# The second layer of a fused attention and snake-activation network: eight units of 576 tokens, and six of 768

## The chip, the cores and the metric

The kernel runs on one core of a Trainium2 chip. The metric is the device time of that core in microseconds, the median of three runs. In the trace PE is TensorE's matmul stream and PEld its loads of stationary operands; DVE is VectorE, ACT ScalarE, POOL GpSimd; SP issues most of the transfers, and ACT issues a few.

## The reference

```python
def _attn_ref(q, k, v):                      # 8 batches, 8 heads, 576 positions, 64 wide
    k_p = k.reshape(B, H, Sp, pool, D).mean(axis=3)
    v_p = v.reshape(B, H, Sp, pool, D).mean(axis=3)
    scores = scale * np.matmul(q, k_p.transpose(0, 1, 3, 2))
    attn = softmax(scores)
    return np.matmul(attn, v_p)
def _moe_ref(x, w_in, w_out, alpha):         # 4608 tokens, 512 -> 2048 -> 512
    h = x @ w_in
    s = np.sin(alpha * h)
    g = h + s * s / (alpha + 1e-09)
    return (g @ w_out).astype(np.float32)
```

All of it is float32. The change concerns the last line alone: `g @ w_out`, a product of 4608 x 2048 by 2048 x 512.

## The kernel before

The first part (`hidden`, `attention`, up to about 514 us) makes g and stores it, transposed, in a scratch tensor `gd` in device memory (`store_g`, L1074). The matmuls of `x @ w_in` have line L848; their moving operand has 256 columns.

The second part is the generator `outputs` (L1290). It takes the 4608 tokens in 8 units of `S` = 576, one for each batch. A unit is one product by a fast scheme of 7 multiplications in place of 8 (Winograd's form of Strassen's), applied twice: an outer level with seven operands numbered 1 to 7 in the `ORDER` 1, 2, 4, 6, 7, 5, 3, and within each of them an inner level with seven again. So a unit has 49 inner products. Each of these adds up four matmuls in PSUM (`product`, L1340), and the profile lists two hardware passes for each float32 matmul: 392 passes a unit, 3136 in all. The moving operand has `T` = `S` / 4 = 144 columns.

The four blocks of a unit's g are loaded by `load_g` (L1286) as tiles r11, r12, r21, r22 (128 partitions x 2304 elements, 1152 KB each). The outer operands are sums of them, made on DVE by `outer`, all with line L1295, since `tt` is defined there: x5 = r21 + r22, x6 = x5 - r11, x7 = r11 - r21 (in r21's place), x3 = r12 - x6; operands 1, 2 and 4 are r11, r12 and r22 as they are. With x5, x6 and x3 these are seven large tiles. For each outer operand `inner` makes four sums s1 to s4 of 576 elements (L1295 too), one product ahead of the matmuls that use them.

The loop at L1427 runs over the (unit, product) pairs, one step for each. A step's stream on PE is: inner product 1 of this pair, then 5 and 4 of the pair before, 6 of this, 2 and 3 of the pair before, 7 of this. (In the first two steps the order differs a little: the first step is mixed into the end of the first layer.) Within the same step DVE gets, in this order: the outer sum that is due, s1 to s3 for the next pair, `combine` of the pair before, s4. So DVE, which works strictly in this order, is tied to PE through `combine`, which reads PSUM.

`combine` (L1370) puts a product's result into the output blocks ca, cb, cc, cd of the pool `op`. Four times a unit `out` (L1357) turns a block by a DVE transpose (L1362) into a tile o (3 buffers) and issues four transfers to the output (L1367, 72 KB each), on SP's queue, and in the last unit on SP's and ACT's in turn (`both`).

The loads of the next unit are all issued on SP's queue: r11, r12 and r22 in the step of product n = 3, r21 in that of n = 5. For unit 0, r11, r12 and r22 are loaded while the first layer still runs (L1560), since their places are free; r21 lies in the pool `gs`, which opens only when the first layer's pools close, and is issued on ACT's queue behind the first layer's last activations (L1571).

Of the kernel before, what the change touches and what calls it, by code (L numbers as in the profile page):

```python
# [40 lines left out]
class Kernel:  # L41
    def __init__(self, tc, q, k, v, w_in, w_out, alpha, out):
        self.tc, self.nc = tc, tc.nc
        self.q, self.k, self.v = q, k, v
        self.w_in, self.w_out, self.alpha, self.out = w_in, w_out, alpha, out
        self.B, self.H, self.S, self.D = q.shape
        self.Sp = self.S // POOL
        self.DM = self.H * self.D
        self.FF = w_in.shape[1]
        self.K1 = self.DM // P  # L50
        self.K2 = self.FF // P
        self.NP = self.H // 2
        self.NU = self.B * self.S // (2 * TH)
        self.NJ = self.K2 // 2 // JW
        self.xT, self.shifts = {}, []
        self.T = self.S // 4

        self.gd = self.nc.dram_tensor("g_bridge", (2, self.NJ * JW, P, self.B * self.S), F32, kind="Internal").ap()

# [1217 lines left out]

    def load_g(self, u, names):  # L1280
        for n in names:
            i, j = divmod(("r11", "r12", "r21", "r22").index(n), 2)
            shape = [P, self.NJ, JW, 2, self.T]
            t = (self.gs if n == "r21" else self.gq if n == "r22" else self.gp).tile(shape, F32, name=n)[:]
            t0 = u * self.S + i * 2 * self.T
            (self.nc.scalar if u == 0 and n == "r21" else self.nc.sync).dma_start(out=t.rearrange("p J b i c -> p (J b) (i c)"),  # L1286
                                   in_=self.gd[j, :, :, t0:t0 + 2 * self.T].rearrange("b p c -> p b c"))
            self.R[n] = t

    def outputs(self):  # L1290
# [9 lines left out]
        def outer(u, n):  # L1300
            r = self.R
            if n == 0:
                X[u] = {1: r["r11"], 2: r["r12"], 4: r["r22"]}
                return
            new = lambda p: self.gs.tile([P, self.NJ, JW, 2, T], F32, name=f"x{p}")[:]
            x = X[u]
            if n == 1:
                x[5] = new(5)
                tt(flat(x[5]), flat(r["r21"]), flat(x[4]), OP.add)
            if n == 2:  # L1310
                x[6] = new(6)
                tt(flat(x[6]), flat(x[5]), flat(x[1]), OP.subtract)
            if n == 3:
                x[7] = r["r21"]
                tt(flat(x[7]), flat(x[1]), flat(x[7]), OP.subtract)
            if n == 4:
                x[3] = new(3)
                tt(flat(x[3]), flat(x[2]), flat(x[6]), OP.subtract)

        def inner(u, n):  # L1320

            x = X[u][ORDER[n]]
            e = self.ne
            self.ne = not e
            new = lambda i: (self.gs if e and i > 1 else self.gq).tile([P, self.NJ, T], F32, name=f"s{i}{int(e)}")[:]
            s1, s2 = new(0), new(1)
            a = lambda i, j: x[:, :, j - 1, i - 1, :]
            tt(s1, a(2, 1), a(2, 2), OP.add)
            tt(s2, s1, a(1, 1), OP.subtract)
            yield  # L1330
            s3, s4 = new(2), new(3)
            tt(s3, a(1, 1), a(2, 1), OP.subtract)
            A[u, n] = {1: a(1, 1), 2: a(1, 2), 3: s4, 4: a(2, 2), 5: s1, 6: s2, 7: s3}
            yield
            tt(s4, a(1, 2), s2, OP.subtract)
# [10 lines left out]
        def early(st):  # L1346

            t = C[st["u"]]["c"]
            with_z(t, st["yz"])
            add(t[:, :, 1], t[:, :, 1], st["x1"][:])  # L1350
            if st["u"] == self.B - 1:
                out(st["u"], 0, 1, t, 5, queues=both)

        def with_z(t, z):
            add(t[:, 1], t[:, 1], z[:, 1:2, :].to_broadcast([P, 2, T]))

        def out(u, i, j, t, n0=0, n1=2 * T // 32, queues=4 * (nc.sync,)):  # L1357

            if n0 or n1 * 32 == 2 * T:
                C[u]["o"] = self.op.tile([P, 2 * T // 32, 2, 32], F32, name="o", bufs=3)  # L1360
            o = C[u]["o"]
            nc.vector.transpose(out=o[:, n0:n1].rearrange("p n h c -> p h n c"),  # L1362
                                in_=t[:].rearrange("p h i c -> p h (i c)").rearrange("p h (n c) -> p h n c", c=32)[:, :, n0:n1])
            r = u * self.S + i * 2 * T
            for a in range(4):
                c = j * 2 * P + a * 64
                queues[a].dma_start(out=self.out[r + 32 * n0:r + 32 * n1, c:c + 64].rearrange("(n k) c -> k n c", k=32),  # L1367
                                        in_=o[32 * a:32 * a + 32, n0:n1].rearrange("k n h c -> k n (h c)"))

        def combine(st):  # L1370

            u, p, x, z = st["u"], st["p"], (st["x0"], st["x1"]), st["yz"]
            c = C.setdefault(u, {})

            def with_x(o, t):
                for i in range(2):
                    add(o[:, :, i], t[:, :, i], x[i][:])
            if p in (1, 4, 5):

                n = "a" if p == 1 else "b"  # L1380
                t = c[n] = block("c" + n)
                for i in range(2):
                    nc.scalar.copy(out=t[:, :, i], in_=x[i][:])
                with_z(t, z)
                if p == 5 and u < self.B - 1:
                    add(c["a"][:], c["a"][:], t[:])
                    out(u, 1, 1, c["a"])
                    add(c["c"][:], c["c"][:], t[:])
                elif p == 5:
                    nc.gpsimd.tensor_tensor(out=c["c"][:], in0=c["c"][:], in1=t[:], op=OP.add)  # L1390
                    add(c["a"][:], c["a"][:], t[:])
                    later.append(lambda: out(u, 1, 1, c["a"], queues=both))
            elif p == 2:
                o = block("cd")
                with_x(o, c["a"])
                with_z(o, z)
                out(u, 0, 0, o)
            elif p == 6:

                t = c["c"] = block("cc")  # L1400
                with_x(t, c["a"])
                with_z(t, z)
            elif p == 7:

                t = c["a"]
                with_x(t, c["c"])
                with_z(t, z)
                add(c["b"][:], c["b"][:], t[:])
                out(u, 1, 0, c["b"])
            else:  # L1410
                t = c["c"]
                add(t[:, :, 0], t[:, :, 0], x[0][:])
                if u < self.B - 1:
                    out(u, 0, 1, t)
                else:
                    out(u, 0, 1, t, 0, 5, both)

        both = 2 * (nc.sync, nc.scalar)
        later = []
        last = None  # L1420
        seq = [(u, n) for u in range(self.B) for n in range(7)]
        outer(0, 0)
        A = {}
        for _ in inner(0, 0):
# [2 lines left out]
        for k in range(len(seq) + 1):  # L1427
            st = None
            if k < len(seq):
                u, n = seq[k]  # L1430
                st = {"u": u, "p": ORDER[n], "A": A.pop((u, n))}
                if 0 < n < 5 and k != 1:
                    outer(u, n)
                if n == 3 and u + 1 < self.B:
                    self.load_g(u + 1, ("r11", "r12", "r22"))
                if n == 5 and u + 1 < self.B:
                    self.load_g(u + 1, ("r21",))
                if n == 6 and u + 1 < self.B:
                    outer(u + 1, 0)
                x0 = st["x0"] = self.bank([P, 2, T])  # L1440
                yz = st["yz"] = self.abank([P, 2, T])
# [51 lines left out]
    def run(self):  # L1493
        nc, tc = self.nc, self.tc
        pool = lambda s, n, b, **kw: s.enter_context(tc.tile_pool(name=n, bufs=b, **kw))
        with ExitStack() as top:
            const = self.const = pool(top, "const", 1)
            self.tp = pool(top, "tp", 1)
            self.PS = pool(top, "ps", 1, space=PSUM).tile([P, 8, 512], F32, name="PS")
            self.aturn = 0  # L1500
            full = self.full = const.tile([P, P], mybir.dt.bfloat16, name="full")
# [3 lines left out]
            engines = {nc.tensor.engine, nc.vector.engine, nc.scalar.engine, nc.gpsimd.engine, nc.sync.engine}  # L1505
            self.wq = pool(top, "wq", 1)
            with ExitStack() as one:
                self.wp = pool(one, "wp", 1)
                self.hp = pool(one, "hp", 2)
                self.xq = pool(one, "xq", 1)  # L1510
                homes = one.enter_context(ExitStack())
                self.xp = pool(homes, "xp", 1)
                att = one.enter_context(ExitStack())
# [31 lines left out]
                for u in range(self.NU):  # L1545
# [8 lines left out]
                            x[i].append(lambda: next(w))  # L1554
                    elif u > self.B - 1:
                        homes.close()
                        self.gq = pool(top, "gq", 1, side="right")
                        for i in (6, 10, 13, 14, 17, 20):
                            x[i].append(lambda: next(w))
                        x[5].append(lambda: self.load_g(0, ("r11", "r12", "r22")))  # L1560
                        for i, f in zip((23, 25, 25, 27), self.inner_w(5, None)):
                            x[i].append(f)
                        o = self.outputs()
                        for i in (22, 25, 27):
                            x[i].append(lambda: next(o))
                    self.hidden(u, x)
                self.end_hidden()
            self.gs = pool(top, "gs", 1, reuse_waits="tile")
            self.op = pool(top, "op", 1, reuse_waits="tile")
# [39 lines left out]
```

## Time and profile before

| | us |
|---|---|
| median of 3 runs | 902.47 (902.22 to 903.03) |
| the profiled execution, its own time | 902.87 |
| its span in the trace | 901.0 |
| PE busy | 894.6 |
| DVE busy | 678.0 |
| ACT busy | 447.9 |
| POOL busy | 212.5 |

A row of the timeline has the start and the length in microseconds, the engine, the line of the source, the operation, output <- input and the count of instructions merged into it; the square brackets say how long the engine was idle before it and who released it. "s" is any inner sum, "r" any loaded tile, "x" any outer operand with a tile of its own. A row of the chain of waits has start, length, engine and line. A row of a table by stages has the stretch, its length, and for each engine the busy time in it and in brackets the number of instructions, then the granted clock, the share of the DMA engines' time and the rate in GB/s. The granted clock of TensorE is 1.00 in all of them.

### The profile page before, as it was taken

How to read it: one execution, taken by the hardware profiler on the slowest of the kernel's cores; microseconds unless marked ns; L12 is line 12 of the kernel's file. 1: busy time of each engine (PE TensorE's matmuls, PEld its weight loads, DVE VectorE, ACT ScalarE, POOL GpSimd, SP SyncE). 2: the span in 40 equal slices, each digit the busy share in tenths (PEclk: the TensorE clock that was granted, in tenths of full speed). 3: DMA queues.
4: the chain of work that ended last, by engine and by line, in shares of the span. 5: the costliest groups of instructions: out<-in, count | busy, mean ns of one | idle time of the engine just before them, and what ended most of it. 6: DMA issues, size and time to landing. Idle time of an engine off the chain costs nothing.

```text
span 901.0 us, 17940 instructions
## 1 busy us (share of the span) xinstructions
PE 894.6 (99%) x7010; PEld 816.3 (91%) x7010; DVE 678.0 (75%) x1010; ACT 447.9 (50%) x1071; POOL 212.5 (24%) x218
## 2 busy tenths in 40 slices
PE   9999999999999999999999999999999999999998
PEld 5787888888888888888888999999999999999997
DVE  7776867768576675764558799979798888889895
ACT  5687776877768777687976611211111111111111
POOL 5698443825337262430000000000000000000000
PEclk9999999999999999999999999999999999999999
DMA  9957957759586585557226346261618172534401
GB/s 264 245 153 206 243 146 210 189 164 253 139 222 184 180 222 145 171 158 282 94 82 223 101 146 191 66 191 35 224 30 230 31 201 64 172 92 127 138 15 40
DMA packets 128371, 141.13 MB, mean 157 GB/s; under 512 B 46416, under 2 KB 95328, under 8 KB 128288
## 3 DMA queue, kind: packets, MB, share of 16 engines
q1 hardware_dynamic: 125504, 137.88, 53.4%
q10 hardware_dynamic: 2784, 2.11, 0.9%
q8 instruction: 56, 0.92, 0.5%
q14 instruction: 27, 0.22, 0.1%
HBM read 75.37 MB, written 47.19 MB: 136 GB/s over the span
## 4 chain that ended last, share of the span: by engine, by line
PE 97%; DVE 2%; DMA 1%; SPq 0%; issue 0%; ACT 0%; DVEq 0%
PE PS L848 46%; PE PS L1340 41%; PE PS L1038 3%; PE PS L317 2%; PE PS L612 2%; PE PS L625 1%; DMA h<-in_v_dram 1%; DVE x L1295 1%; DVE s L1295 0%; DVE r L1295 0%; PE PS L568 0%; PE PS L570 0%; PE PS L289 0%; PE PS L278 0%; PE PS L478 0%; SPq L164 0%
## 5 line engine op out<-in xcount | busy, mean ns | idle before, releaser
L848 PE MATMUL PS<-home,a 128*128 128x256 f32 x1104 | 258.1, 381 | 0.1
L848 PEld LDWEIGHTS PS<-home,a 128*128 128x128 f32 x1104 | 205.3, 190 | 32.3 <-issue 4.6
L848 PE MATMUL PS<-home,as 128*128 128x256 f32 x768 | 182.6, 381 | 0.0
L848 PEld LDWEIGHTS PS<-home,as 128*128 128x128 f32 x768 | 141.8, 190 | 19.7 <-ACT PS L822 1.2
L1390 POOL TENSOR_TENSOR cc<-cc,cb 128x576 f32<-128x576 f32 x1 | 2.0, 1977 | 501.7 <-DVE cb L1295 501.7
L1340 PE MATMUL PS<-s,wb 128*128 128x144 f32 x896 | 119.1, 286 | 0.0
L1340 PEld LDWEIGHTS PS<-s,wb 128*128 128x128 f32 x896 | 113.7, 190 | 0.1
L1015 ACT ACTIVATE s<-s,c 128x256 f32<-128x256 f32 (+1 forms) x228 | 113.5, 565 | 0.0
L821 DVE TENSOR_TENSOR h<-PS,p 128x512 f32<-128x512 f32 x72 | 49.3, 684 | 64.0 <-PE PS L848 37.4
L131 POOL TENSOR_TENSOR kvin<-kvin 96x768 f32<-96x768 f32 (+3 forms) x42 | 73.8, 1756 | 70.3 <-DMA kvin<-in_v_dram 68.1
L1468 ACT COPY PS<-PS 128x144 f32<-128x144 f32 x56 | 14.7, 263 | 145.0 <-PE PS L1340 138.4
L1008 ACT ACTIVATE s<-h,al 128x256 f32<-128x256 f32 x144 | 65.6, 509 | 38.3 <-DVE h L821 38.3
L1340 PE MATMUL PS<-r,wb 128*128 128x144 f32 x512 | 73.3, 286 | 0.3 <-DVE r L1295 0.3
L1340 PE MATMUL PS<-s,a 128*128 128x144 f32 x512 | 73.2, 286 | 0.0
L1008 ACT ACTIVATE s<-PS,al 128x256 f32<-128x256 f32 x144 | 60.2, 471 | 18.8 <-PE PS L848 17.9
L1060 DVE TENSOR_TENSOR h<-PS,s 128x512 f32<-128x512 f32 x36 | 24.8, 689 | 57.4 <-ACT s L1015 57.4
L1340 PEld LDWEIGHTS PS<-r,wb 128*128 128x128 f32 x512 | 67.1, 190 | 0.5 <-DVE r L1295 0.5
L1340 PEld LDWEIGHTS PS<-s,a 128*128 128x128 f32 x512 | 67.1, 190 | 0.0
L822 ACT COPY PS<-PS 128x512 f32<-128x512 f32 x72 | 41.5, 576 | 35.4 <-PE PS L848 30.6
L1488 ACT COPY PS<-PS 128x144 f32<-128x144 f32 x56 | 14.7, 263 | 88.1 <-PE PS L1340 88.1
L1340 PE MATMUL PS<-x,wb 128*128 128x144 f32 x384 | 54.9, 286 | 0.0
L1340 PE MATMUL PS<-s,we 128*128 128x144 f32 x384 | 54.9, 286 | 0.0
(216 smaller groups left out, 1407.5 us busy)
## 6 DMA issues: line engine op xcount, KB each, us to landing
g_bridge<-h SPq DMA_DIRECT2D x72, 512.0 KB
r<-g_bridge SPq DMA_DIRECT2D x31, 1152.0 KB
out_dram<-o SPq DMA_DIRECT2D x122, 72.0 KB
kvin<-in_k_dram SPq DMA_DIRECT2D x14, 576.0 KB
q<-in_q_dram SPq DMA_DIRECT2D x7, 1024.0 KB
kvin<-in_v_dram SPq DMA_DIRECT2D x14, 512.0 KB
aM<-tr SPq DMA_DIRECT2D x54, 92.0 KB
aM<-tr SPq DMA_DIRECT2D x54, 88.0 KB
```

The costliest lines, as they stand in the source:

```text
L131: self.nc.gpsimd.tensor_tensor(out=t[..., 0:w] if w > D else out, in0=t[..., 0:w], in1=t[..., w:2 * w], op=OP.add)
L317: nc.tensor.matmul(ps[e][r0 + r:r0 + r + q.shape[-1], h, :], q[s], kb[s, hp, :], start=True, stop=True)
L612: nc.tensor.matmul(o[r:r + 64], w, x, start=start and i < 2, stop=False, skip_group_check=True)
L821: add = lambda o, x, y: nc.vector.tensor_tensor(out=o, in0=x, in1=y, op=OP.add)
L822: copy = lambda o, x: nc.scalar.copy(out=o, in_=x)
L848: nc.tensor.matmul(ps[:, jj, :], self.A[p][:, kk, f * P:(f + 1) * P], x[:, kk, :], start=(start and n == 0), stop=(kk == 1), skip_group_ch ...
L1008: self.nc.scalar.activation(out=G.s[:, i, jj, j, :], in_=src[:, jj], func=AF.Sin, scale=self.al[:, f:f + 1])
L1015: self.nc.scalar.activation(out=x, in_=x, func=AF.Square, scale=self.c[:, f:f + 1])
L1038: nc.tensor.matmul(o, W[m][:, G.J - J0], X[m], start=start and n == 0, stop=True, skip_group_check=True)
L1060: add = lambda o, x, y: self.nc.vector.tensor_tensor(out=o, in0=x, in1=y, op=OP.add)
L1340: nc.tensor.matmul(out, W[:, J // 2, J % 2, :], A[:, J, :], start=(start and J == 0), stop=(J == self.NJ - 1), skip_group_check=True)
L1468: nc.scalar.copy(out=x1[:, 0, :], in_=x0[:, 1, :])
```

## The change

The units are made of 768 tokens: 6 in place of 8, with T = 192, so a matmul's moving operand has 192 columns, a large tile 3072 elements (1536 KB), an inner sum 768. As larger tiles have to fit in the same memory:

- seven large tiles become six. x3 is now made in r12's place; in unit 0, x5 is made in r21's place and x7 takes the tile called x5. From then on names change places from unit to unit (`big`): r12 of the next unit is loaded into the tile that x6 leaves, and so on.
- unit 0 makes x6 in two steps, (r22 - r11) + r21, and x5 as r21 + r22 later: five outer sums in place of four, in an order of their own.
- r22 has a pool of its own, gx, in the place of the first layer's last tiles. Its load for unit 0 no longer runs during the first layer: it is issued on SP's queue when the first layer's last matmul has been done (`L1597` of the changed file). r21's is issued on ACT's queue as before.
- the loads of a later unit go one per product: r11, r22, r12, r21 in the steps n = 3, 4, 5, 6. Unit 1's go r11, none, r12, then r22 and r21 together.
- o has 1 buffer in place of 3, cd is gone (its work is done in cc), and the last half block of the output is turned into the place of r11.
- the last unit's last block is put out in two halves of 6 groups of 32 tokens, where it was 5 and 4.

```diff
-        self.T = self.S // 4
+        self.NO = 6
+        self.T = self.B * self.S // (4 * self.NO)
...
+    def big(self, n, u):
+
+        if u % 2:
+            n = {"r12": "x6", "x6": "r12"}.get(n, n)
+        if u:
+            n = {"r21": "x5", "x5": "r21"}.get(n, n)
+        return (self.gp if n in ("r11", "r12") else self.gx if n == "r22" else self.gs).tile([P, self.NJ, JW, 2, self.T], F32, name=n)[:]
...
-            t0 = u * self.S + i * 2 * self.T
+            t = self.big(n, u)
+            t0 = u * 4 * self.T + i * 2 * self.T
...
         def outer(u, n):
             r = self.R
             if n == 0:
-                X[u] = {1: r["r11"], 2: r["r12"], 4: r["r22"]}
+                X[u] = {1: r["r11"], 2: r["r12"]}
                 return
+            x, op = X[u], lambda o, a, b, f: tt(flat(o), flat(a), flat(b), f)
+            if u == 0:
+                if n == 1:
+                    x[6] = self.big("x6", u)
+                    op(x[6], x[4], x[1], OP.subtract)
+                if n == 2:
+                    op(x[6], x[6], r["r21"], OP.add)
+                if n == 3:
+                    x[7], x[5] = self.big("x5", u), r["r21"]
+                    op(x[7], x[1], r["r21"], OP.subtract)
+                if n == 4:
+                    op(x[5], x[5], x[4], OP.add)
+            else:
+                if n == 1:
+                    x[5] = self.big("x5", u)
+                    op(x[5], r["r21"], r["r22"], OP.add)
+                if n == 2:
+                    x[6] = self.big("x6", u)
+                    op(x[6], x[5], x[1], OP.subtract)
+                if n == 3:
+                    x[7] = r["r21"]
+                    op(x[7], x[1], x[7], OP.subtract)
+            if n == (4 if u else 5):
+                x[3] = x[2]
+                op(x[3], x[2], x[6], OP.subtract)
...
+            def new(i):
+                y = e and not (i == 1 and (u, n) == (0, 1))
+                return (self.gs if y and i else self.gq).tile([P, self.NJ, T], F32, name=f"s{i}{int(y)}")[:]
...
-            if n0 or n1 * 32 == 2 * T:
-                C[u]["o"] = self.op.tile([P, 2 * T // 32, 2, 32], F32, name="o", bufs=3)
+            if n0:
+                o = C[u]["o"] = self.big("r11", u).rearrange("p J b i c -> p (J b i c)")[:, 0:4 * T].rearrange("p (n h c) -> p n h c", h=2, c=32)
+            elif n1 * 32 == 2 * T:
+                C[u]["o"] = self.op.tile([P, 2 * T // 32, 2, 32], F32, name="o", bufs=1)
...
-                o = block("cd")
+                o = block("cc")
...
-        seq = [(u, n) for u in range(self.B) for n in range(7)]
+        seq = [(u, n) for u in range(self.NO) for n in range(7)]
+        first_loads = ("r11",), (), ("r12",), ("r22", "r21")
+        later_loads = ("r11",), ("r22",), ("r12",), ("r21",)
...
-                if 0 < n < 5 and k != 1:
+                if 0 < n < 6 and k != 1:
                     outer(u, n)
-                if n == 3 and u + 1 < self.B:
-                    self.load_g(u + 1, ("r11", "r12", "r22"))
-                if n == 5 and u + 1 < self.B:
-                    self.load_g(u + 1, ("r21",))
+                if n > 2 and u + 1 < self.NO:
+                    self.load_g(u + 1, (later_loads if u else first_loads)[n - 3])
...
-                        x[5].append(lambda: self.load_g(0, ("r11", "r12", "r22")))
+                        x[5].append(lambda: self.load_g(0, ("r11", "r12")))
...
+                homes.close()
+                self.gx = pool(top, "gx", 1, side="right")
+                self.load_g(0, ("r22",))
                 self.end_hidden()
```

More of the change, by code (lines that the diff above doesn't have):

```diff
@@ L1282, in load_g @@
             i, j = divmod(("r11", "r12", "r21", "r22").index(n), 2)
-            shape = [P, self.NJ, JW, 2, self.T]
-            t = (self.gs if n == "r21" else self.gq if n == "r22" else self.gp).tile(shape, F32, name=n)[:]
-            t0 = u * self.S + i * 2 * self.T
+            t = self.big(n, u)
+            t0 = u * 4 * self.T + i * 2 * self.T
             (self.nc.scalar if u == 0 and n == "r21" else self.nc.sync).dma_start(out=t.rearrange("p J b i c -> p (J b) (i c)"),
@@ L1302, in outer, with inner @@
             if n == 0:
-                X[u] = {1: r["r11"], 2: r["r12"], 4: r["r22"]}
+                X[u] = {1: r["r11"], 2: r["r12"]}
                 return
[L1305 to L1309, printed above, removed]
-            if n == 2:
[L1311 to L1320, printed above, removed]
+            x, op = X[u], lambda o, a, b, f: tt(flat(o), flat(a), flat(b), f)
[23 more added lines that the diff above has]
+                op(x[3], x[2], x[6], OP.subtract)
+        def inner(u, n):
+            if n == 2:
+                X[u][4] = self.R["r22"]
             x = X[u][ORDER[n]]
@@ L1324, in inner @@
             self.ne = not e
-            new = lambda i: (self.gs if e and i > 1 else self.gq).tile([P, self.NJ, T], F32, name=f"s{i}{int(e)}")[:]
+            def new(i):
+                y = e and not (i == 1 and (u, n) == (0, 1))
+                return (self.gs if y and i else self.gq).tile([P, self.NJ, T], F32, name=f"s{i}{int(y)}")[:]
             s1, s2 = new(0), new(1)
@@ L1350, in early @@
             add(t[:, :, 1], t[:, :, 1], st["x1"][:])
-            if st["u"] == self.B - 1:
-                out(st["u"], 0, 1, t, 5, queues=both)
+            if st["u"] == self.NO - 1:
+                out(st["u"], 0, 1, t, T // 32, queues=both)
         def with_z(t, z):
@@ L1363, in out @@
                                 in_=t[:].rearrange("p h i c -> p h (i c)").rearrange("p h (n c) -> p h n c", c=32)[:, :, n0:n1])
-            r = u * self.S + i * 2 * T
+            r = (2 * u + i) * 2 * T
             for a in range(4):
@@ L1384, in combine @@
                 with_z(t, z)
-                if p == 5 and u < self.B - 1:
+                if p == 5 and u < self.NO - 1:
                     add(c["a"][:], c["a"][:], t[:])
@@ L1412, in combine @@
                 add(t[:, :, 0], t[:, :, 0], x[0][:])
-                if u < self.B - 1:
+                if u < self.NO - 1:
                     out(u, 0, 1, t)
                 else:
-                    out(u, 0, 1, t, 0, 5, both)
+                    out(u, 0, 1, t, 0, T // 32, both)
         both = 2 * (nc.sync, nc.scalar)
@@ L1431, in outputs @@
                 st = {"u": u, "p": ORDER[n], "A": A.pop((u, n))}
-                if 0 < n < 5 and k != 1:
+                if 0 < n < 6 and k != 1:
                     outer(u, n)
-                if n == 3 and u + 1 < self.B:
-                    self.load_g(u + 1, ("r11", "r12", "r22"))
-                if n == 5 and u + 1 < self.B:
-                    self.load_g(u + 1, ("r21",))
-                if n == 6 and u + 1 < self.B:
+                if n > 2 and u + 1 < self.NO:
+                    self.load_g(u + 1, (later_loads if u else first_loads)[n - 3])
+                if n == 6 and u + 1 < self.NO:
                     outer(u + 1, 0)
@@ L1497, in run @@
             const = self.const = pool(top, "const", 1)
-            self.tp = pool(top, "tp", 1)
             self.PS = pool(top, "ps", 1, space=PSUM).tile([P, 8, 512], F32, name="PS")
@@ L1507, in run @@
             with ExitStack() as one:
+                self.tp = pool(one, "tp", 1)
                 self.wp = pool(one, "wp", 1)
                 self.hp = pool(one, "hp", 2)
-                self.xq = pool(one, "xq", 1)
+                rest_homes = one.enter_context(ExitStack())
+                self.xq = pool(rest_homes, "xq", 1)
                 homes = one.enter_context(ExitStack())
@@ L1556, in run @@
                         homes.close()
+                        homes = rest_homes
                         self.gq = pool(top, "gq", 1, side="right")
```

## The prediction

> **What bounds the kernel now.** I read the page first, then the chain of waits in order of time, then the timelines of PE, DVE, ACT and SP around 506 to 536 us.
>
> ```profile
> PE 894.6 (99%) x7010; PEld 816.3 (91%) x7010; DVE 678.0 (75%) x1010; ACT 447.9 (50%) x1071; POOL 212.5 (24%) x218
> PE 97%; DVE 2%; DMA 1%; SPq 0%; issue 0%; ACT 0%; DVEq 0%
> ...
> 523.25 2.48 DVE x L1295
> ...
> 533.31 2.48 DVE r L1295
> 535.79 0.04 issue
> 535.83 360.92 PE PS L1340 x2944
> 896.75 0.02 issue
> 896.77 0.47 DVE cc L1295
> ...
> 897.26 0.51 DVE o L1362
> ```
>
> PE is the bound: the chain runs through it for 97%, and from 535.83 us to 896.75 in one piece. So the second layer costs what its passes cost, and only two other places count: unit 0, where the chain goes through DVE's outer sums, and the 4.25 us behind the last pass.
>
> **The passes.** What a pass costs shows at two widths. The first rows are SP's queue, where the same load opens each unit; the others are PE's rows of the first layer.
>
> ```profile
> 581.61 14.66 SPq L1286 DMA_DIRECT2D r<-g_bridge  x4
> ...
> 725.66 14.66 SPq L1286 DMA_DIRECT2D r<-g_bridge  x4
> ...
> 413.46 3.62 PE L848 MATMUL PS<-home,a 128*128 128x256 f32 x16
> ...
> 447.99 1.89 PE L848 MATMUL PS<-home,as 128*128 128x256 f32 x8
> ```
>
> 144.05 us are three units of 392 passes: 122.49 ns for 144 columns. Between the two L848 rows lie 160 passes (nine rows of 16, two of 8): 215.8 ns for 256 columns. The line through both is 0.833 ns a column and 2.5 ns a pass, so 192 columns cost 162.5 ns. Columns times passes don't change (3136 x 144 = 2352 x 192); 784 passes fewer save 784 x 2.5 = 1.96 us. Bounds: were the 2.5 ns at 144 columns all due to the weight loads (PEld is as busy as PE there), 192 columns would cost 160 and 7.9 us go; were the cost in proportion to the columns, nothing. I take the line: PEld is far from always busy at 256 columns (816.3 over the whole against PE's 894.6), and there is the same 2.5 ns.
>
> **Unit 0, before.** DVE starts on the sums of r22 at 520.01 and hands over x7, in r21's place, just late:
>
> ```profile
> 520.01 0.75 DVE L1295 TENSOR_TENSOR s<-r 128x576 f32<-128x576 f32 x1
> ...
> 523.17 2.55 DVE L1295 TENSOR_TENSOR x<-r,r 128x2304 f32<-128x2304 f32 x1
> 525.76 2.56 DVE L1295 TENSOR_TENSOR x<-x,r 128x2304 f32<-128x2304 f32 x1
> 528.42 0.76 DVE L1295 TENSOR_TENSOR s<-x 128x576 f32<-128x576 f32 x1
> ...
> 533.23 2.55 DVE L1295 TENSOR_TENSOR r<-r,r 128x2304 f32<-128x2304 f32 x1
> ...
> 533.44 2.12 PE L1340 MATMUL PS<-s,wb 128*128 128x144 f32 x16
> 535.83 1.25 PE L1340 MATMUL PS<-r,wb 128*128 128x144 f32 x8 [0.27 <-DVE r L1295]
> ```
>
> 16 passes from 533.44 end their turn at 535.40, so PE lost 0.43 us. The new kernel has the same stages here with larger tiles, x6 in two steps where x5 and x6 were, then x7. Two widths give DVE's price: (2.55 - 0.75) / 1728 = 1.04 ns an element, so a sum of 576 grows by 0.20 us at 768, one of 2304 by 0.80 at 3072, a result of 288 by 0.10 and a transpose by 0.2. Call L the time from which r22 can be used. L to the first x6 step: 523.17 - 520.01 = 3.16, four sums and one result more, 4.06. That step 2.59 + 0.80 = 3.39, the second 2.66 + 0.80 = 3.46 up to the next start, 0.1 less to its end. From there to x7, 4.81 + 4 x 0.20 + 3 x 0.10 + 0.2 = 6.11, and x7 to PE 2.60 + 0.80 = 3.40. So x6 is there at L + 10.81, x7 at L + 20.42.
>
> PE's side:
>
> ```profile
> 506.70 1.14 PE L1340 MATMUL PS<-r,wb 128*128 128x144 f32 x8
> ...
> 512.11 1.89 PE L848 MATMUL PS<-home,a 128*128 128x256 f32 x8
> 513.84 1.14 PE L1340 MATMUL PS<-s,wb 128*128 128x144 f32 x8
> ...
> 514.04 0.84 ACT L1008 ACTIVATE s<-PS,al 128x256 f32<-128x256 f32 x2 [0.23 <-PE PS L848]
> 514.77 0.51 ACT L1015 ACTIVATE s<-s,c 128x256 f32<-128x256 f32 x1
> 514.92 0.39 ACTq L1286 DMA_DIRECT2D r<-g_bridge  x1
> ```
>
> Two groups of 8 passes lie between 506.70 and 513.84; each grows from 0.98 to 1.30, so the first layer's last pass gives way at 514.48 and its result is out at 514.68 (ACT got it 0.20 behind). One group on, then steps of seven groups, 9.10 us: r22 is wanted at 524.88, x6 at 533.98, x7 at 543.08. The wait for DVE sums to S = L - 522.66 where that is positive.
>
> **L, the moved load.** Before, r22 came while the first layer ran, under cover of PE. Now SP issues it at 514.7, and ACT issues r21 at about 515.56: its place is behind the second activation of 514.04, which moves by 0.64. r21 before is the nearest row for the price, alone on the engines:
>
> ```profile
> 515.00:515.80 0.80, 0.80 (x8) 0.80 (x8) 0.00 (x0) 0.80 (x3) 0.00 (x0) 1.00 0.00 0
> 515.80:516.80 1.00, 1.00 (x11) 1.00 (x10) 0.00 (x0) 1.00 (x3) 0.00 (x0) 1.00 1.09 43
> ...
> 519.00:520.00 1.00, 1.00 (x11) 1.00 (x10) 1.00 (x2) 0.02 (x1) 0.00 (x0) 1.00 1.08 391
> ...
> q10 hardware_dynamic: 1040, 1.18, 91.7%
> q1 hardware_dynamic: 93, 0.19, 10.0%
> ```
>
> The last but one is ACT's queue from 515.9 to 520.8 us: 1.18 MB were in 5.9 us after the issue, at 391 GB/s once running. 0.39 MB more take 1.0: r22 alone is in at 514.7 + 6.9 = 521.6, and with 0.3 for the signal (PE's to ACT took 0.2) L = 521.9, which gives S = 0 with 0.8 to spare. But r21, 0.9 us behind, wants the same engines. How two queues share shows in the last transfers of the output, each 72 KB or 288 packets, on SP's queue (q1) and ACT's (q10); three stretches of 0.4 us from 895.5:
>
> ```profile
> q1 hardware_dynamic: 229, 0.06, 66.6%
> q10 hardware_dynamic: 31, 0.01, 8.9%
> ...
> q10 hardware_dynamic: 180, 0.05, 64.6%
> q1 hardware_dynamic: 74, 0.02, 20.1%
> ...
> q1 hardware_dynamic: 231, 0.06, 64.7%
> q10 hardware_dynamic: 142, 0.03, 43.7%
> ```
>
> They take turns, but by whole transfers. If that holds for a load of 1024 packets, r22, first in, is served first, and S = 0. I take this; the upper bound is that all 3.15 MB come in together (514.7 + 5.9 + 1.97 MB / 391 GB/s = 525.6), and beyond it the first layer's last store, 1.05 MB, ahead too: 528.3.
>
> The Trainium skill ("DMA: Bandwidth & Descriptors", Queues, rings and completion order) says that each DMA engine goes round between the queues with work packet by packet, typically 9 to 17 descriptors at a time. By that r22's 64 a engine would alternate with r21's, and the time would be that of the first rival below. The rows above agree with turns; their 288 packets are 18 an engine, so they can't tell a turn of 18 from one of 64.
>
> **The rest.** Behind the last pass the two last DVE steps grow by 0.10 and 0.07 (320 to 384 elements), and the last four transfers from 40 to 48 KB: +0.3 us in all; the upper bound is that all 768 packets more of the last two blocks come serially, at 757 a microsecond (1211 in the four stretches of which three are shown), +1.0. The later units' loads and the single o tile cost nothing as long as DVE's lead covers them: before, x6 of unit 2 was ready 3.3 us early (below), and DVE is idle for 7 of 48 us. r21, one step later than before, has the four transfers of one output block and 6.9 us of its own ahead, 9 of the 18 us until x5 reads it. An output block is wanted out of o 9.1 us behind its issue and needs 1.9 to issue and about 2 to move. Fewer, larger DVE operations only add to the lead.
>
> ```profile
> 629.63:677.65 48.02, 48.02 (x394) 48.02 (x393) 41.05 (x54) 8.47 (x27) 0.00 (x0) 1.00 0.41 124
> ...
> 619.25 2.55 DVE L1295 TENSOR_TENSOR x<-x,r 128x2304 f32<-128x2304 f32 x1
> ...
> 625.12 1.14 PE L1340 MATMUL PS<-x,wb 128*128 128x144 f32 x8
> ```
>
> Sum: 901.0 - 1.96 - 0.43 + 0.3 = 898.9 for the span; 902.87 - 901.0 = 1.87 lies around it, and the profiled execution was 0.40 above the median: 900.4 us.
>
> **The rivals.** First: the loads share. r22 is then done about a quarter of r21 (1.0 us) before 525.6, L = 524.9, S = 2.2: 902.6 us, the saving spent. For it: r21 comes 0.9 us behind on another queue; against it, the whole turns above.
>
> Second, and slower: r22 comes last, behind r21 and the first layer's last store. L = 525.9 with r21 alone ahead, 528.6 with the store too; S = 3.2 to 5.9, 903.6 to 906.3, say 905. It is slower than before from L = 524.7 on. For it: SP's first packets of that store (q1 above) already meet the end of r21; against it, r22 is issued first and the store behind it on the same queue.
>
> Third: the change saves nothing per pass, because the cost goes with the columns. Then only -0.43 + 0.3 is left: 902.3. Against it, two widths with the same 2.5 ns.
>
> Fourth: the 2.5 ns were the weight loads', and go wholly: 1.96 becomes 7.9, 894.5 us. The 256-column row speaks against it.
>
> **How the numbers follow.** Forecast 0.52 (its own range 899.7 to 901.3), sharing 0.22, r22 last 0.14, nothing saved 0.06, weight loads 0.02, and 0.04 for a stall at a unit's border that I don't see. A measurement here tells 0.2%, 1.8 us, from no change: faster is below 900.67, slower above 904.27. Two thirds of the forecast and the fourth rival are faster, 0.37; the rest of the forecast, most of the sharing and the third, 0.43; r22 last, what sharing costs beyond its sum, and the unseen stall, 0.20. The range goes from 899.7 to 904.6, which leaves out half of the slow rival, the fourth and a little of the forecast.
>
> **What would show it.** The unit's distance on SP's queue should be 63.7 us and PE without a gap in it. In unit 0, DVE's sum of r22 should start by 522 us; a DVE idle from 521.3 until 525 and PE waiting 2 us for x6 and x7 together would be the first rival, 528 the second. Passes of 163.3 ns would be the third. The prediction is wrong if PE waits at a later unit's x6, or if DVE's transposes wait for the output transfers.

## The result, and the profile after

| | before | after |
|---|---|---|
| median, us | 902.53 (901.85 to 903.53, 16 runs) | 901.04 (900.40 to 902.59, 16 runs) |
| ratio, 95% interval | | 0.9982 (0.9975 to 0.9990) |
| profiled execution, us | 902.87 | 901.13 |
| its span, us | 901.0 | 899.3 |

The kernel is 1.5 us faster, 0.18%; the interval lies below 1, so the gain is clear of noise, though less than the 0.2% from which the prediction called a time faster. The forecast was 900.4 us, 0.6 below the measured median, which lies in the forecast's own range (to 901.3). The page's first part and the chain of waits of the changed kernel stand against the same rows of before:

```profile
PE 892.8 (99%) x6226; PEld 814.6 (91%) x6226; DVE 670.7 (75%) x903; ACT 440.4 (49%) x1017; POOL 213.2 (24%) x218
PE 95%; DVE 2%; DMA 2%; SPq 0%; issue 0%; ACT 0%; DVEq 0%
...
514.70 8.07 DMA r<-g_bridge
...
522.86 0.97 DVE s L1303
...
527.09 3.28 DVE x L1303
...
530.39 3.37 DVE x L1303
...
540.05 3.28 DVE x L1303
543.33 0.04 issue
543.37 351.28 PE PS L1364 x2160
894.65 0.02 issue
894.67 0.56 DVE cc L1303
...
895.26 0.58 DVE r L1388
```

The chain again ends in one piece of PE, now from 543.37 to 894.65: 2160 passes at 162.6 ns. In it PE waits for nothing, at no border of two units either. SP's queue gives the same price by another route. These are two loads of one tile name, one unit apart:

```profile
757.41 0.44 SPq L1294 DMA_DIRECT2D x<-g_bridge  x1
...
821.10 0.44 SPq L1294 DMA_DIRECT2D x<-g_bridge  x1
```

63.69 us for 392 passes, 162.5 ns.

What is new stands ahead of it. From 514.70 to 522.77 the chain goes through r22's load, and from there through DVE's sums to x7. The timeline of the changed kernel (DVE, then PE) shows what is left of it on PE:

```profile
520.21 0.95 DVE L1303 TENSOR_TENSOR s<-r,s 128x768 f32<-128x768 f32 x1
522.86 0.96 DVE L1303 TENSOR_TENSOR s<-r 128x768 f32<-128x768 f32 x1 [1.71 <-DMA r<-g_bridge]
...
524.91 1.46 PE L1364 MATMUL PS<-r,wb 128*128 128x192 f32 x8
...
534.01 1.46 PE L1364 MATMUL PS<-x,wb 128*128 128x192 f32 x8
...
540.51 2.76 PE L1364 MATMUL PS<-s,wb 128*128 128x192 f32 x16
543.37 1.57 PE L1364 MATMUL PS<-x,wb 128*128 128x192 f32 x8
```

DVE stood idle for 1.71 us, until r22 was there. PE started r22 at 524.91 and x6 at 534.01 without a wait; x7 was due at 540.51 + 2.60 = 543.11 and came at 543.37, 0.26 late (0.43 before).

So the account of the spans is: passes, 2944 at 122.6 ns (360.92 us) against 2160 at 162.6, which over all 3136 and 2352 makes -2.0; the stall in unit 0 -0.17; behind the last pass 899.3 - 894.65 = 4.65 against 4.25, +0.4. Sum -1.8, measured 899.3 - 901.0 = -1.7.

### The profile page after: what moved, and what is told of

Same layout as the page of the kernel before. It is cut to its first block, busy times and chain, and to the rows that moved or that the text cites. A ratio compares the mean times of both kernels' runs of the same rounds, so it can differ in the third digit from the quotient of the medians.

```text
span 899.3 us, 16070 instructions
## 1 busy us (share of the span) xinstructions
PE 892.8 (99%) x6226; PEld 814.6 (91%) x6226; DVE 670.7 (75%) x903; ACT 440.4 (49%) x1017; POOL 213.2 (24%) x218
## 4 chain that ended last, share of the span: by engine, by line
PE 95%; DVE 2%; DMA 2%; SPq 0%; issue 0%; ACT 0%; DVEq 0%
PE PS L849 46%; PE PS L1364 39%; PE PS L1039 3%; PE PS L318 2%; PE PS L613 2%; DVE x L1303 1%; DMA r<-g_bridge 1%; PE PS L626 1%; DMA h<-in_v_dram 1%; DVE s L1303 1%; PE PS L569 0%; PE PS L571 0%; PE PS L290 0%; PE PS L279 0%; DVE cc L1303 0%
## 5 line engine op out<-in xcount | busy, mean ns | idle before, releaser
L1416 POOL TENSOR_TENSOR cc<-cc,cb 128x768 f32<-128x768 f32 x1 | 2.6, 2584 | 498.3 <-DVE cb L1303 498.3
L1364 PE MATMUL PS<-s,wb 128*128 128x192 f32 x672 | 116.2, 326 | 0.0
L1364 PEld LDWEIGHTS PS<-s,wb 128*128 128x128 f32 x672 | 110.4, 190 | 0.1
L1494 ACT COPY PS<-PS 128x192 f32<-128x192 f32 x42 | 12.7, 303 | 145.3 <-PE PS L1364 133.4
L1364 PE MATMUL PS<-r,wb 128*128 128x192 f32 x432 | 79.0, 326 | 0.0
L1364 PEld LDWEIGHTS PS<-r,wb 128*128 128x128 f32 x432 | 71.7, 190 | 0.1
L1364 PE MATMUL PS<-s,a 128*128 128x192 f32 x384 | 70.2, 326 | 0.0
L1364 PEld LDWEIGHTS PS<-s,a 128*128 128x128 f32 x384 | 63.7, 190 | 0.0
L1514 ACT COPY PS<-PS 128x192 f32<-128x192 f32 x42 | 12.7, 303 | 89.5 <-PE PS L1364 89.5
L1303 DVE TENSOR_TENSOR s<-r 128x768 f32<-128x768 f32 x54 | 51.4, 952 | 5.1 <-PE PS L1364 2.8
L1061 DVE TENSOR_TENSOR h<-h,s 128x1024 f32<-128x1024 f32 x36 | 53.3, 1482 | 1.1 <-ACT s L1016 0.9
```

The lines of the kernel that those rows point to most:

```text
L1061: add = lambda o, x, y: self.nc.vector.tensor_tensor(out=o, in0=x, in1=y, op=OP.add)
L1303: tt = lambda o, x, y, op: nc.vector.tensor_tensor(out=o, in0=x, in1=y, op=op)
L1364: nc.tensor.matmul(out, W[:, J // 2, J % 2, :], A[:, J, :], start=(start and J == 0), stop=(J == self.NJ - 1), skip_group_check=True)
```

## The experiments

What remained to be told apart: why r22 was usable 1.0 us later than forecast; whether the gain is the width's or the staging's; whether the prices of zero in the prediction (single o tile, loads one per product, tile places) are zero; and how far the price of a pass follows the line.

| run | median, us | runs | against before, 95% interval |
|---|---|---|---|
| changed kernel | 901.04 | 16 | 0.9982 (0.9975 to 0.9990) |
| r21_on_sp | 900.75 | 11 | 0.9979 (0.9970 to 0.9987) |
| r22_last | 907.29 | 4 | 1.0053 (1.0038 to 1.0069) |
| before_o1 | 903.88 | 10 | 1.0017 (1.0008 to 1.0026) |
| units_8 | 906.26 | 5 | 1.0042 (1.0029 to 1.0054) |
| u8_place | 904.39 | 11 | 1.0017 (1.0008 to 1.0026) |
| u8_place_o3 | 903.18 | 11 | 1.0005 (0.9996 to 1.0013) |
| units_9 | 916.90 | 4 | 1.0161 (1.0147 to 1.0175) |
| pass_96 | 848.47 | 1 | part of the work left out |

### r21_on_sp: the second load out of the way

```diff
-            (self.nc.scalar if u == 0 and n == "r21" else self.nc.sync).dma_start(out=t.rearrange("p J b i c -> p (J b) (i c)"),
+            self.nc.sync.dma_start(out=t.rearrange("p J b i c -> p (J b) (i c)"),
```

> The changed kernel with unit 0's r21 load on SP's queue, behind r22 and the first layer's last store, in place of ACT's queue. In the trace of the changed kernel DVE could use r22 from 522.86 us (L), 0.9 later than forecast. If that 0.9 is what r21 takes from r22 on another queue, r22 is alone now: L = 521.4 to 521.9, no wait of PE for DVE in unit 0 (0.26 us before), and r21, in by about 528, is still ahead of the second x6 step that reads it (from about 529.4). Time: 0.2 to 0.3 us under the changed kernel, about 900.8 against 901.0 us. If the 0.9 has another cause (the load itself is as slow as that, or its signal), L stays at 522.8 and the time at 901.0. If r21 is late behind the store (rival on the other side), the second x6 step waits for it beyond 530.4 and PE waits the same time more at x6 or x7: 901.3 or above.

Measured: 900.75 us, span 899.0 (changed kernel 899.3). The queues' rows in the stretch from 519.4 to 521.6 us, first of the changed kernel (SP's queue is q1, ACT's q10; packets, MB, share of the engines), then of this run:

```profile
q1 hardware_dynamic: 314, 0.48, 60.9%
q10 hardware_dynamic: 228, 0.35, 45.3%
```

```profile
q1 hardware_dynamic: 515, 0.86, 105.6%
```

The same 2.2 us carried r22 and r21 side by side there and SP's queue alone here. What became of it, in the timeline of DVE and in the chain of this run:

```profile
521.57 0.96 DVE L1303 TENSOR_TENSOR s<-r 128x768 f32<-128x768 f32 x1 [0.31 <-DMA r<-g_bridge]
...
529.53 3.36 DVE L1303 TENSOR_TENSOR x<-x,r 128x3072 f32<-128x3072 f32 x1
...
514.77 379.61 PE PS L1364 x2336
```

DVE has r22 at 521.57 instead of 522.86 and waits 0.31 us for it instead of 1.71; the step that reads r21 at 529.53 has no wait. The chain is one piece of PE from 514.77, the first pass behind the first layer's last, to 894.38: no stall is left. Both numbers of the theory hold (L and the 0.3 us), so the delay of L was r21's part of the engines. Of the medians alone, 900.75 and 901.04, this couldn't be said, since their intervals overlap; it rests on the traces. The median of r21_on_sp is the lowest of the runs that do the whole work.

### r22_last: the slow rival, built

```diff
-            (self.nc.scalar if u == 0 and n == "r21" else self.nc.sync).dma_start(out=t.rearrange("p J b i c -> p (J b) (i c)"),
+            (self.nc.scalar if u == 0 and n in ("r21", "r22") else self.nc.sync).dma_start(out=t.rearrange("p J b i c -> p (J b) (i c)"),
...
-                self.load_g(0, ("r22",))
...
-                self.load_g(0, ("r21",))
+                self.load_g(0, ("r21", "r22"))
```

> The changed kernel with unit 0's r22 load on ACT's queue behind r21, so that r22 is the last of the two for certain. This builds the second rival of the prediction on purpose. Price by its formula S = L - 522.66: both loads are in at about 526.8 us (when r21 landed in the changed kernel's trace), or up to 528.2 with the first layer's last store between them, so S = 4.1 to 5.5, and the time is 3.9 to 5.2 us above the changed kernel: 904.9 to 906.2 us. If DVE's lead were larger than the formula says (that is, if the step times of the prediction are wrong), the time would be nearer 901 to 903.

Measured: 907.29 us, 6.25 above the changed kernel: beyond the upper end. The chain, then PE's timeline, then the table by stages (stretch, its length, busy time of PE, PEld, DVE, ACT and POOL with counts, granted clock, DMA share, GB/s):

```profile
515.70 13.03 DMA r<-g_bridge
528.74 0.14 issue
528.87 371.97 PE PS L1364 x2272
```

```profile
528.87 2.90 PE L1364 MATMUL PS<-r,wb 128*128 128x192 f32 x8 [4.11 <-DMA r<-g_bridge]
531.56 2.67 PE L1364 MATMUL PS<-s,we 128*128 128x192 f32 x8
534.07 1.46 PE L1364 MATMUL PS<-r,we 128*128 128x192 f32 x8
```

```profile
524.70:528.80 4.10, 0.06 (x1) 0.00 (x0) 0.00 (x0) 0.30 (x1) 0.00 (x0) 0.80 0.87 331
528.80:532.60 3.80, 3.73 (x12) 3.76 (x13) 3.67 (x5) 0.46 (x1) 0.00 (x0) 0.50 0.02 4
532.60:540.00 7.40, 7.40 (x43) 7.40 (x42) 7.26 (x4) 0.30 (x1) 0.00 (x0) 0.91 0.00 0
```

L was 528.74, half a microsecond beyond the expected end. By the formula S = L - 522.66 PE would lose 6.1 us, 5.8 more than the changed kernel's 0.26. It lost 6.6, made up otherwise: 4.11 us waiting for r22 itself, whose place in PE's stream comes ahead of x6 and x7, and 371.97 - 2272 x 0.1626 = 2.5 us after it, because the clock went to half: 16 passes cost 5.2 us in place of 2.6. When PE came to x7, at 549.67, DVE had it (since 545.93 + 3.35 = 549.28). At full clock PE would have been there 2.5 us sooner, at 547.2, and would have waited 2.1 us. So the formula, which looks at DVE's results alone, had the sum nearly right, 4.1 + 2.1; the slow clock, which it left out, mostly took the place of the wait for x7 and cost some 0.4 us beyond it, by an estimate from these rows. L's half microsecond and this are most of the 1.1 us beyond the upper end.

### before_o1: one o tile in the kernel before

```diff
-                C[u]["o"] = self.op.tile([P, 2 * T // 32, 2, 32], F32, name="o", bufs=3)
+                C[u]["o"] = self.op.tile([P, 2 * T // 32, 2, 32], F32, name="o", bufs=1)
```

> The kernel before with one o tile in place of three, the only edit. The prediction costs the single tile at nothing, covered by DVE's lead of 3.3 us: then the time is that of the kernel before, 902.5 us, with DVE waiting for the output transfers in the trace (a few us at a unit's border) and PE waiting for nothing new. If the lead doesn't cover it, PE waits at each of the 7 borders, and 1 us each would make 909.

Measured: 903.88 us, 1.3 us slower, span 902.3. PE waits for nothing new at a border, but the end is longer. The same transpose in the kernel before and in this run:

```profile
896.23 0.45 DVE L1362 STREAM_TRANSPOSE o<-cc 128x256 f32<-128x256 f32 x1
```

```profile
897.59 0.45 DVE L1362 STREAM_TRANSPOSE o<-cc 128x256 f32<-128x256 f32 x1 [1.41 <-DMA out_dram<-o]
```

Behind PE's last pass nothing covers a wait: the transpose has to stand until the block before it has left the tile. The changed kernel doesn't pay this, because it puts the last half blocks in r11's place (`big("r11", u)` in `out`): its 0.58 us transpose at 895.26 in the chain above follows its DVE sum at once. The single tile without that line costs 1.3 us in the kernel before; the prediction, which had the single tile covered by DVE's lead, left out that behind PE's end there is no lead.

### units_8: the change without its width

```diff
-        self.NO = 6
+        self.NO = 8
```

> The changed kernel with 8 units of 576 tokens again: 144 columns a pass and 3136 passes, but with the moved r22 load, x6 in two steps, six large tiles, the single o tile. It does the change without its width. If the gain is the passes' (1.97 us), it goes here: a pass takes 122.5 ns, a unit 48.02 us. r22 of 0.88 MB is in at L = 520.3 to 520.9, the tiles are smaller and PE wants them sooner: x7 comes at L + 15.8 and is wanted at 535.4, S = 0.7 to 1.3. With the tail of before: 902.8 to 903.5 us, no gain left over before, or 0.3 to 1 us worse. If the gain came from the staging (loads, tiles, x6 in two steps) and not from the width, the time stays near 901.0.

Not shown in the edit: the two lines that split the last unit's last block round the half up, since 288 columns are nine groups of 32. The runs named u8 below have this too.

Measured: 906.26 us, 3.7 above before and 2.8 above the expected end. The passes do cost 122.6 ns. PE's waits in this run, and the two rows of the list of waits that the next two runs test as their causes (us in total, times, longest):

```profile
524.68 1.25 PE L1364 MATMUL PS<-r,we 128*128 128x144 f32 x8 [0.54 <-ACT PS L1514]
...
530.72 1.25 PE L1364 MATMUL PS<-x,wb 128*128 128x144 f32 x8 [0.87 <-DVE x L1303]
...
538.18 1.25 PE L1364 MATMUL PS<-x,wb 128*128 128x144 f32 x8 [0.34 <-DVE x L1303]
...
576.32 1.22 PE L1364 MATMUL PS<-s,a 128*128 128x144 f32 x8 [0.63 <-DVE s L1303]
...
587.86 1.25 PE L1364 MATMUL PS<-x,wb 128*128 128x144 f32 x8 [0.33 <-DVE x L1303]
```

```profile
ACT ca L1409 <- DMA g_bridge<-h: 3.2, 1, 3.2
...
DVE o L1388 <- DMA out_dram<-o: 3.0, 1, 3.0
```

ACT's copy of unit 0's first product into ca waits 3.2 us for the first layer's last store: with tiles of 576 the pools are smaller, and ca comes to lie where that store reads. In the changed kernel the list of waits has no such row. And at the first border the transpose waits 3.0 us for the single o tile. The changed kernel has that row too, and PE doesn't notice:

```profile
DVE o L1388 <- DMA out_dram<-o: 2.8, 1, 2.8
```

It is the border at which r22 and r21 of the next unit go out together (in units_8 at 560.33 and 560.91 us), ahead of a block's output transfers on the same queue (563.07); at the later borders the program issues one load per product, and no transpose waits.

Two runs take these waits away one after the other.

### u8_place and u8_place_o3: the two waits taken away

```diff
+            pool(top, "pad", 1).tile([P, 3072], F32, name="pad")
             self.op = pool(top, "op", 1, reuse_waits="tile")
...
-                C[u]["o"] = self.op.tile([P, 2 * T // 32, 2, 32], F32, name="o", bufs=1)
+                C[u]["o"] = self.op.tile([P, 2 * T // 32, 2, 32], F32, name="o", bufs=3)
```

Both start from units_8. The first line (12 KB left free) alone is u8_place, both changes are u8_place_o3.

> 8 units of 576 again, with one more edit: 12 KB left free ahead of the pool of output blocks, so that unit 0's first block (ca) no longer lies where the first layer's last results are stored from. In the 8-unit run ACT's copy into ca waited 3.2 us for that store (until 523.75 us), DVE stood idle 1.86 us for ca, and PE lost 2.2 us in unit 0 (0.70, 1.03 and 0.50) and 1.4 us at the border to unit 1, where the transpose waited 3.0 us for the single o tile. Theory: ca's place cost most of unit 0's share; without it only x7 stays late, 0.5 to 0.6 us, and 1.4 us of the o tile remain: 904.3 to 904.8 us. If the place costs nothing by itself (r22's transfer or DVE's steps set the pace), the time stays at 906.3.

> The kernel of u8_place with three o tiles again (they fit at 576 tokens). Theory: both waits of the 8-unit run are gone and only x7 in unit 0 comes late, 0.5 to 1.3 us: 902.8 to 903.5 us, the value first expected of 8 units: the staging without its two placement costs is worth nothing, and the gain over before is the width's. If the o tile costs nothing by itself, as in the kernel before with one o tile, the time is that of u8_place.

Measured: 904.39 and 903.18 us, both inside what was expected; in this staging and at 576 tokens, the place of ca costs 1.9 us and the single o tile 1.2. The chain of u8_place_o3 is then that of the kernel before, to the length of its last piece of PE:

```profile
533.55 2.48 DVE x L1303
536.03 0.04 issue
536.07 360.92 PE PS L1364 x2944
```

Its ratio to before, 1.0005 (0.9996 to 1.0013), is no difference that can be measured. So the staging by itself, without its two waits, gains nothing that can be measured, and the 2.1 us from here to the changed kernel's 901.04 are the width's, 2.0 of them the passes' by the traces.

### units_9 and pass_96: where the line ends

```diff
-        self.NO = 6
+        self.NO = 9
```

```diff
-                nc.tensor.matmul(out, W[:, J // 2, J % 2, :], A[:, J, :], ...
+                nc.tensor.matmul(out[:, 0:96], W[:, J // 2, J % 2, :], A[:, J, 0:96], ...
```

> The changed kernel with 9 units of 512 tokens: 128 columns a pass and 3528 passes. By the line of the prediction (0.833 ns a column and 2.5 ns a pass) a pass takes 109.2 ns and a unit of 392 passes 42.8 us, so that all passes take 385.1 us, 1.0 more than at 144 columns. With the waits that the 8-unit run showed (ca's place, the o tile): 907 to 908 us. In proportion to the columns (162.6 / 192 = 0.847 ns each) a pass would take 108.4 ns and a unit 42.5 us. If the weight loads set a pace between 109 and 122 ns, the unit takes longer than 42.8 us, up to 48, and the time goes up by as much as 46 us.

> The changed kernel with only the first 96 of the 192 columns in each pass of the second layer; the other half of each result is left out. It measures one pass where nothing was measured: by the line 0.833 x 96 + 2.5 = 82.5 ns, so 8 passes in a row start 0.66 us apart from the next 8; in proportion to the columns 81.3. If weight loads set a floor under the 109 to 122 ns of the narrowest passes measured, the 8 take longer than 0.66 us, up to 0.98. The unit itself will be set by DVE (some 53 us busy in 63.7), so its length says nothing on a pass.

Measured: units_9 916.9 us, 9 above what the line gave. In pass_96 half the columns took the time from 901 to 848 us only, since PE then often waits for DVE and part of the passes run at half the clock (last section). PE's timeline of units_9, seven steps of 56 passes apart, and of pass_96, one such step without a wait in it:

```profile
643.66 1.06 PE L1364 MATMUL PS<-r,wb 128*128 128x128 f32 x8
...
687.44 1.06 PE L1364 MATMUL PS<-r,wb 128*128 128x128 f32 x8
```

```profile
567.91 1.06 PE L1364 MATMUL PS<-r,wb 128*128 128x96 f32 x8
...
574.16 1.06 PE L1364 MATMUL PS<-x,wb 128*128 128x96 f32 x8
```

43.78 us / 392 = 111.7 ns with 128 columns, 6.25 / 56 = 111.6 with 96. The line gives 109.2 and 82.5. So at these two widths a pass costs the same; each pass has one load of a 128 x 128 operand, which doesn't change with the columns, so this is most simply the load's pace (nothing that was run changes the load itself). By the line, 111.6 ns are reached at (111.6 - 2.5) / 0.833 = 131 columns; that is an estimate, since nothing between 128 and 144 was run. The 2.5 ns that a pass of 128 columns takes above the line (111.7 against 109.2) make 8.8 us in 3528 passes, the miss of units_9.

## Why the prediction was right, point by point

- **The passes.** Forecast 162.5 ns and -1.96 us; measured 162.5 to 162.6 ns and -2.0. 192 lies between the two widths that the line was drawn through. Against its fourth rival (the 2.5 ns are the weight loads') the prediction took "the same 2.5 ns" at 256 columns as evidence. It is none, since a line through two points has one intercept by construction; the third width decides. 192 columns took neither 160 ns (that rival's price) nor 161.9 (in proportion to the 215.8 of 256 columns) nor 163.3 (in proportion to 144, the third rival). There is a floor, but at 111.6 ns, below the 122.5 of 144 columns. That the gain is the width's and not the staging's, u8_place_o3 shows.
- **L, the moved load.** The step that was off. It said that r22, first in, is served first as a whole, usable at 521.9. r22 was served alone at first, but not to its end: in the changed kernel SP's queue was alone until 519.3 us, and then the two shared, so that L was 522.86. Its price alone was right to 0.3 us: with no second queue (r21_on_sp) it was usable at 521.57. L so went a third of the way from the forecast's 521.9 to the first rival's 524.9. That the miss of 1.0 us cost only 0.26 is due to the 0.8 us that the forecast had to spare: the time came out well although the assumption of whole turns was wrong for this load.
- **DVE's steps from L to x7.** Forecast L + 20.42, with L = 522.86 543.28; PE had it at 543.37. S by the formula 0.20, measured 0.26.
- **Behind the last pass.** Forecast +0.3, measured +0.4. DVE's part is as forecast (0.56 + 0.58 against 0.47 + 0.51, +0.16), the transfers grew by 0.2 where 0.13 was taken.
- **The prices of zero.** On PE they held in the changed kernel. But one sign that the prediction had named for being wrong did come: DVE's transpose waited for the output transfers, once, 2.8 us at the first border. The prediction's time for emptying the o tile (1.9 us to issue, about 2 to move) didn't count the two loads that lie ahead on the queue there; that they are the cause is likely, but no run takes them away. DVE's lead covered the wait, as the prediction said of the tile's price; beside it and r22's in unit 0, the list of waits has no new one of DVE or PE for a transfer. The zero depends on the width: in the same staging at 576 tokens the o tile costs 1.2 us and the place of ca 1.9. It depends on the staging too: in the kernel before, at 576 tokens, the single tile cost PE nothing at the borders (before_o1). At the end, where no lead covers, the zero is the work of r11's place.
- **The sum.** 898.9 forecast for the span, 899.3 measured; the 0.4 are S (0.26) and the end (0.1).

The section of the Trainium skill that the prediction weighed ("DMA: Bandwidth & Descriptors", Queues, rings and completion order: engines go round between the queues, some 9 to 17 descriptors at a time) fits the second half of the overlap and not the first. From 519.4 to 521.6 us the two queues had 314 and 228 packets, as turns shorter than a whole load would give (the size of a turn doesn't show). But ahead of that ACT's queue got nothing for some 3.8 us after its issue (below), while r22 had some 42 of the 64 packets of each engine behind it. Whether r21's packets were ready for the engines by then, no run shows.

## What to carry to other kernels

Where an operand's width can be chosen, measure the pass at two widths in the trace and look for the floor: here the fixed part was worth 2.0 us of 900 from 144 to 192 columns, while 16 columns fewer than 144 cost some 10 us of passes (3528 x 111.7 ns against 3136 x 122.6). A tile that is reused costs nothing only where something covers it: ask of each shared place what runs behind the last pass, and which earlier transfer still reads there; both answers change with the tile's size. Of two loads with different due times, try the later one behind the earlier one on the same queue: on a queue of its own it took engines from the earlier one here and made it 1.3 us later (522.86 against 521.57).

## What the runs showed of the hardware that was not expected

**A second queue starts late, then takes about half.** In the changed kernel ACT issues r21 at 515.59 us. In the queues' rows of the stretch from 515.6 to 519.3 us there is only SP's queue; from 523 to 526, r21 and the first layer's last store divide the time about evenly:

```profile
515.59 0.39 ACTq L1294 DMA_DIRECT2D r<-g_bridge  x1
```

```profile
q1 hardware_dynamic: 670, 1.03, 80.8%
...
q10 hardware_dynamic: 392, 0.60, 54.7%
q1 hardware_dynamic: 298, 0.58, 50.2%
```

In the kernel before, where it was alone, the same issue (514.92) had its first packets in the stretch from 515.8. It isn't a matter of ACT's queue: in r22_last, where ACT's queue had both loads, SP issued the store at 519.13, and from 519.2 to 522.8 us there were 881 packets of ACT's queue and none of SP's; from 523 to 526 it was 361 and 333. What decides when a second queue comes in wasn't tried.

**The clock falls behind waits of PE, and not only behind those of 4 us.** In r22_last 4.11 us without a pass were followed by 3.8 us at a granted clock of 0.50. In pass_96, where PE often waits, a wait of 4.43 us had the same effect. Shorter ones did it too. Behind a wait of 2.08 us the passes still ran at full pace; but after one more of 1.42 us the granted clock was 0.50 from 564.4 to 567.4 us, and 16 passes took 3.31 us where they take 1.95 at full clock:

```profile
532.66 2.02 PE L1364 MATMUL PS<-x,wb 128*128 128x96 f32 x8 [4.43 <-DVE x L1303]
...
558.32 1.13 PE L1364 MATMUL PS<-r,wb 128*128 128x96 f32 x8 [2.08 <-DVE r L1303]
...
562.66 1.10 PE L1364 MATMUL PS<-s,we 128*128 128x96 f32 x8 [1.42 <-DVE we L743]
...
564.76 3.31 PE L1364 MATMUL PS<-s,wb 128*128 128x96 f32 x16
```

Nor does the length of the last wait decide: of two waits of 1.59 us in this run, the one that ended at 700.45 was followed by passes at 0.50, and the one that ended at 806.81 by passes at 1.00. What does decide isn't shown. The Trainium skill ("TensorE: Matmul & The Clock Gate", HAM oscillation) tells to leave no gaps over about 3.4 us between matmuls, since TensorE then starts again at half its clock. The waits of 4.11 and 4.43 us agree; the shorter ones show that to stay below that length wasn't enough here. Such a stretch isn't lost in full where PE would wait anyway: in r22_last it took 2.5 us, 2.1 of them in the place of a wait for x7.

**A pass has a floor** of 111.6 ns at 96 and at 128 columns, with the granted clock at 1.00.
